# Two edits to a fused state-space mixer and MLP kernel: zero-padded bias rows, and a reordered opening

## The chip, the cores and the metric

The kernel runs on one core of one Trainium2 chip. The metric is device time in microseconds (us) of one execution; lower is better. The kernel before was run 7 times: median 574.7 us, from 574.32 to 580.91. One further number matters below: the execution that the profiler recorded took 574.59 us.

## What is computed

The input x has 2048 rows (tokens) of 1024 features. Two branches are computed from it and mixed by a gate per token:

```
g = sigmoid((x * gate_w).sum(-1))
a = S5(x):   Bu = x @ B_bar^T (complex);  h_t = Lam_bar * h_(t-1) + Bu_t;  a = 2 Re(h @ C^T) + x * Dskip
b = MLP(x):  gelu(layernorm(x) @ w1 + b1) @ w2 + b2        (1024 -> 3584 -> 1024)
out = g * a + (1 - g) * b
```

The bias b2 is a row of 1024 numbers that is added to every token's row of the second MLP product. In the kernel it is added on TensorE.

## The kernel before, in words

All work is recorded as tasks with an engine, an estimated duration, a priority and what they read and write. A planner (`Graph.schedule`) plays the tasks through its own estimates, and so fixes, before anything runs, one order of instructions for each engine: TensorE (PE), VectorE (DVE), ScalarE (ACT), GpSimd (POOL) and SyncE (SP, which issues most of the loads). On the chip each engine goes through its list in that order and waits at semaphores for what others must have done first. So an edit to a few tasks can move the order of many others.

The matrix products are done by a fast scheme with seven block products in place of eight. A group (`SG`) has seven parts `p1` to `p7`, each a run of K accumulating matmuls of 128x512 into a PSUM bank (`mm`, the matmuls of L828, which open an accumulation, and of L830, which add to one). Parts are interleaved between groups: a group's last parts run within the next group. Each group needs sums and differences of its operand blocks, which DVE makes (`dve_tt`, L882), and its results are moved out of PSUM by ACT and DVE.

The stages, in order of time:

- The **opening** (0 to about 25 us). SP issues loads of 128 rows each: rows of B (real and imaginary parts, `load_b`, L633 and L634) and of x (`load_x`, L621). PE transposes them with an identity, eight 128x128 transposes for one load: `t_x` for the first four loads of x (L650), `t_b` for the first four pairs of B (L666). Each set of eight fills one PSUM bank; DVE empties it for x (L654), ACT for B (L670). The banks come from `tbank()`, which gives bank 7 and bank 3 in turn. A row of small constants is transposed as well (`cst_T`, L684) and copied by DVE (L693); a chain of small DVE instructions on these constants follows. The first products of x and B (`bu_plain`) are woven in between the transposes of B, and `z_gate` (L1033, into bank 7) makes the gate's sums.
- The **bu stage** (to about 118 us): 14 groups of 28 matmuls, x times B. Meanwhile ACT, DVE and POOL do the layer norm, and DVE makes tables for the scan (L768).
- Four pairs of **m** and **b** stages (to about 468 us). An m stage is the first MLP product with gelu: 7 groups of 28 matmuls; DVE adds at L1275, ACT applies the gelu at L1271 and L1277. A b stage is the second product: 4 groups of 49 matmuls; DVE ends them at L1357. The first two pairs belong to the first half of the hidden features (`Fh == 0`), and only there b2 is added. In this time DVE also does the scan of the state-space branch (L1142, L1145, L1156), in 16 units, as filling between the work that PE waits for.
- The **y stage** (to the end): 8 groups of 56 matmuls with the scanned states and C, then out.

How b2 gets in: in each b group of the first half, part `p1` and part `p5` have one more matmul than the others. In `p1` its stationary operand is one row of 128 ones and its moving operand one row with the first half of b2; in `p5` they are two rows: (1, -1) and the two halves of b2. Both stationary operands are the first row or rows of the small tile STG, which `signs` (POOL, L687) overwrites once the constants have been transposed; the b2 rows lie in the buffer B2B, filled by two small loads (`em_b2`, L1557 and L1558). The lines:

```
v_one = View(V(STG, 0, [(1, 128)], npart=1), [b_stg])
v_sgn = View(V(STG, 0, [(1, 128)], npart=2), [b_stg])
st["A11"], mv["B11"] = st["A11"] + [v_one], mv["B11"] + [v_b2l]
st["S1"], mv["T1"] = st["S1"] + [v_sgn], mv["T1"] + [v_b2r]
```

B2B has had another use by then: the bu stage keeps one of its sums there (`US5`).

Of the kernel before, what the change touches and what calls it, by code (L numbers as in the profile page):

```python
# [412 lines left out]
def V(t, off, dims, npart=128):  # L413
    ps = 1
    for s in t.shape[1:]:
        ps *= s
    return bass.AP(t, off, [[ps, npart]] + [[a, b] for (a, b) in dims])


def build(nc, A_x, A_Lambda_re, A_Lambda_im, A_B_re, A_B_im, A_C_re, A_C_im, A_log_dt, A_Dskip,  # L420
          B_x, B_w1, B_b1, B_w2, B_b2, gate_w, out, stats=None):
    x2 = A_x[0]
    out2 = out[0]
    L, D = x2.shape
# [4 lines left out]
    DT = D // 128  # L429
# [14 lines left out]
    g = Graph()  # L444
    es = ExitStack()
    with es:
# [5 lines left out]
        def sem(name, dram=False):  # L452
            nsem[0] += 1
            return SemC(es.enter_context(nc.semaphore(name)), name, dram)
# [9 lines left out]
        STG = sb("stg", [128, 128], BF16)  # L464
        IDENT = sb("ident", [128, 128], BF16)
        ONESF = sb("onesf", [128, 128], F32)
# [61 lines left out]
        def tbank():  # L528
            return (7, 3)[nxt("tbank", 2)]
# [96 lines left out]
        def load_b(pt, prio):  # L626
            s = pt % 4

            v = AR.v(RX + s * 4096, [(1, 2 * D)])
            BN[pt] = v  # L630

            def em(e, pt=pt, s=s):
                i1 = e.dma_start(out=AR.v(RX + s * 4096, [(1, D)]).ap, in_=A_B_re[pt * 128:(pt + 1) * 128, :])  # L633
                i2 = e.dma_start(out=AR.v(RX + s * 4096 + 2048, [(1, D)]).ap, in_=A_B_im[pt * 128:(pt + 1) * 128, :])  # L634
                return [i1, i2]
            g.dma(prio, em, 2 * 128 * D * 2, ssem("bnat", s), writes=[v], name="bnat%d" % pt, ndma=2)
# [1 line left out]
        first_e = []  # L638
        first_a = []

        def t_x(k, prio):
            bk = tbank()
            v = XNAT[k]

            def em(e, k=k, bk=bk):
                ins = None
                base = XNAT[k].ap
                for dt in range(DT):
                    src = AR.v(XOFF(k) + dt * 256, [(1, 128)]).ap
                    ins = e.transpose(V(PS16[bk], dt * 128, [(1, 128)]), src, V(IDENT, 0, [(1, 128)]))  # L650
                return ins
            g.add("pe", 0.06 * DT, prio, em, reads=[v, b_ident], writes=[b_ps[bk]], name="xT_T%d" % k)
            o = AR.v(xqo(0, 0) + k * 256, [(512, DT), (1, 128)])
            first_e.append(g.add("dve", 0.65, prio, lambda e: e.tensor_copy(o.ap, V(PS16[bk], 0, [(128, DT), (1, 128)])),  # L654
                                 reads=[b_ps[bk]], writes=[o, b_ps[bk]], name="xT_e%d" % k))

        def t_b(pt, prio):
            s = pt % 4
            for ri in range(2):
                bk = tbank()  # L660

                def em(e, ri=ri, bk=bk):
                    ins = None
                    for dt in range(DT):
                        src = AR.v(RX + s * 4096 + ri * 2048 + dt * 256, [(1, 128)]).ap
                        ins = e.transpose(V(PS16[bk], dt * 128, [(1, 128)]), src, V(IDENT, 0, [(1, 128)]))  # L666
                    return ins
                g.add("pe", 0.06 * DT, prio, em, reads=[BN[pt], b_ident], writes=[b_ps[bk]], name="bT%d.%d" % (pt, ri))
                o = AR.v(bqo(pt, 2 * ri), [(1, D)])
                first_a.append(g.add("act", c_act(D), prio, lambda e, o=o, bk=bk: e.activation(o.ap, V(PS16[bk], 0, [(1, D)]), AF.Copy),  # L670
                                     reads=[b_ps[bk]], writes=[o, b_ps[bk]], name="bTe%d.%d" % (pt, ri)))

        load_b(0, (-0.95, 0))
        for k in range(4):
            load_x(k, (-0.9, k))
        for pt in range(1, 4):
            load_b(pt, (-0.85, pt))

        for k in range(4):
            t_x(k, (-0.8, k))  # L680
        t_b(0, (-0.79, 0))
        bk0 = tbank()
        g.add("pe", 0.06, (-0.75, 0),
              lambda e: e.transpose(V(PS16[bk0], 0, [(1, NROW)]), V(STG, 0, [(1, 128)], npart=NROW), V(IDENT, 0, [(1, NROW)], npart=NROW)),  # L684
              reads=[b_stg, b_ident], writes=[b_ps[bk0]], name="cst_T", extra=[g.tasks[-2]])
        g.add("pool", 0.4, P0,
              lambda e: e.affine_select(V(STG, 0, [(1, 128)], npart=2), V(ONESF, 0, [(1, 128)], npart=2), [[0, 128]], ALU.is_equal, -1.0,  # L687
                                        base=0, channel_multiplier=1),
              reads=[b_ones], writes=[b_stg], name="signs").slack = 4.0
        v_one = View(V(STG, 0, [(1, 128)], npart=1), [b_stg])  # L690
        v_sgn = View(V(STG, 0, [(1, 128)], npart=2), [b_stg])
        stage_names = ["LRE", "LIM", "LDT", "DSK", "B2", "GW", "B1"]
        cst_cp = g.add("dve", 0.15, P0, lambda e: e.tensor_copy(V(CST, 0, [(1, NROW)]), V(PS16[bk0], 0, [(1, NROW)])),  # L693
              reads=[b_ps[bk0]], writes=[bc(n) for n in stage_names] + [b_ps[bk0]], name="cst_copy")
# [484 lines left out]
        NP2 = FT // 4  # L1179
        b_acs = [B("acs%d" % k) for k in range(NTT)]  # L1180
        b_w1s = [B("w1s%d" % j) for j in range(FT // 2)]
        v_b2l = AR.v(B2B, [(1, 512)], npart=1)
        v_b2r = AR.v(B2B + 1024, [(1, 512)], npart=2)

        def xq(i, dt=None):
            if dt is None:
# [140 lines left out]
        def b_group(Fh, c, tp):  # L1327
            def hq(kh, t):
                return [ht(kh * HF + k, (2 * tp + t) * 128, 128) for k in range(HF)]

            def sq(i):
                return [AR.v(SQ + (tp + 1) % 2 * 7168 + i * 1792 + k * 256, [(1, 128)], FP16) for k in range(HF)]
            st = {"A11": hq(0, 0), "A12": hq(1, 0), "A22": hq(1, 1), "S1": sq(0), "S2": sq(1), "S3": sq(2), "S4": sq(3)}
            f = lambda i: [wq(i, k) for k in range(HF)]
            mv = {"B11": f(0), "B21": f(1), "B22": f(2), "T1": f(3), "T2": f(4), "T3": f(5), "T4": f(6)}
            if Fh == 0:

                st["A11"], mv["B11"] = st["A11"] + [v_one], mv["B11"] + [v_b2l]
                st["S1"], mv["T1"] = st["S1"] + [v_sgn], mv["T1"] + [v_b2r]
            o0 = [AO + nxt("bao", 4) * 4096 for _ in range(2)]  # L1340
            ov = [AR.v(o0[i // 2] + (i % 2) * 2048, [(1, 512)], F32) for i in range(4)]
            s5 = AR.v(AO + 16384, [(1, 512)], F32)
            k0 = c * 8 + 2 * tp
            gm = [(C("GM1", k0 + t), bc("GM1")) for t in range(2)]
            done = {}

            def fin(qd, q, bk):
                t = qd // 2
                o = ov[qd]
                nm = "%d.%d.%d" % (Fh, k0 // 2, qd)  # L1350
                sc = gm[t]
                sv = o if qd == 1 else s5
                if qd % 2 == 0:
                    g.add("act", c_act(512, ap_operands=1), (10.0, q + 1), lambda e: e.activation(o.ap, V(PS[bk], 0, [(1, 512)]), AF.Copy, scale=sc[0]),  # L1354
                          reads=[b_ps[bk], sc[1]], writes=[o, b_ps[bk]], name="ac" + nm)
                else:
                    g.add("dve", c_dve(512), (10.0, q - 2), lambda e: e.scalar_tensor_tensor(o.ap, V(PS[bk], 0, [(1, 512)]), sc[0], sv.ap, ALU.mult, ALU.add),  # L1357
                          reads=[b_ps[bk], sc[1], sv], writes=[o, b_ps[bk]], name="ac" + nm)
                done[qd] = True
                k = k0 + t  # L1360
                if done.get(2 * t) and done.get(2 * t + 1):
                    av = AR.v(o0[t], [(1, D)], F32)
                    if Fh == 0:
                        g.dma((10.0, q + 2), lambda e: e.dma_start(out=ACS[k], in_=av.ap), 128 * D * 4, ssem("ao", k % 4, True), reads=[av], writes=[b_acs[k]], name="acs%d.%d" % (Fh, k), q="pool")  # L1364
                    else:
                        g.dma((10.0, q + 2), lambda e: e.dma_start(out=ACS[k], in_=av.ap, accum_op=ALU.add), 128 * D * 4, ssem("ao", k % 4, True), reads=[av, b_acs[k]], writes=[b_acs[k]], name="acs%d.%d" % (Fh, k), q="pool")  # L1366
            return SG("_b%d.%d" % (Fh, k0 // 2), st, mv, fin, ov[1], s5, sc=[gm[0], gm[1]])
# [140 lines left out]
        for n, it in enumerate(flat):  # L1508
# [46 lines left out]
            if n == 0:  # L1555
                def em_b2(e):
                    return [e.dma_start(out=AR.v(B2B, [(1, D)], npart=1).ap, in_=bass.AP(B_b2.tensor, B_b2.offset, [[0, 1], [1, D]])),  # L1557
                            e.dma_start(out=AR.v(B2B + 1024, [(1, 512)], npart=1, p0=1).ap, in_=bass.AP(B_b2.tensor, B_b2.offset, [[0, 1], [1, 512]]))]  # L1558
                g.dma((40.0, 0), em_b2, 4096, sem("d_b2b"), writes=[v_b2l, v_b2r], name="b2b", ndma=2)
                w2_load(0)  # L1560
                for pg in range(PG):
                    for q in range(NQ):
                        ssm(pg, q)
# [80 lines left out]
```

## Time and profile before

| | |
|---|---|
| median of 7 runs | 574.7 us |
| the profiled execution: its own time / span from first to last instruction | 574.59 / 572.9 us |
| PE busy | 552.5 us, 96% of the span |
| DVE busy | 511.7 us, 89% |
| ACT busy | 279.7 us, 49% |
| POOL busy | 99.1 us, 17% |
| first transpose on PE | starts at 5.02 us |
| last matmul's result taken up by DVE | 565.65 us |

The busy time of PE counts overlapping matmuls once, and the end of a matmul is modelled, so the distance from one start to the next is the better measure of what a matmul costs. In the timeline, several like instructions are merged into one row: start, time from the first's start to the last's end, engine, line, and a count. A record can be missing.

### The profile page before, as it was taken

The numbers are of one execution on the slowest core, as the hardware profiler recorded it, in microseconds if no ns is written. First come the engines' busy times: TensorE is split into PE (matmuls) and PEld (weight loads), VectorE is DVE, ScalarE is ACT, GpSimd is POOL, SyncE is SP. The second block draws the span as 40 slices with busy tenths as digits, with TensorE's granted clock in tenths as the row PEclk, the third lists the DMA queues.
The fourth block names the chain that finished last, engine by engine and source line by source line (L and its number), as shares of the span: only waits on it lengthen the run. The fifth ranks groups of instructions, "written<-read, shape, count | busy, mean of one in ns | idle before, by whom it ended". The sixth has DMA issues, their size and how long they took to land.

```text
span 572.9 us, 7432 instructions
## 1 busy us (share of the span) xinstructions
PE 552.5 (96%) x2569; PEld 249.3 (44%) x2617; DVE 511.7 (89%) x865; ACT 279.7 (49%) x465; POOL 99.1 (17%) x159
## 2 busy tenths in 40 slices
PE   5899999999999999999999999999999999999994
PEld 4444444444334444444434444444444444444442
DVE  3899999999999999999999999999995878998652
ACT  2978999667652247662236673336662321111110
POOL 0024856630101010001211000210000210011000
PEclk9999999999999999999999999999999999999998
DMA  9975999889994766403878999899579999777501
GB/s 283 261 248 111 287 309 316 265 285 282 370 258 134 262 245 225 146 33 115 263 297 289 339 281 217 215 272 276 183 147 244 313 315 279 255 237 268 176 37 55
DMA packets 116675, 134.50 MB, mean 235 GB/s; under 512 B 70548, under 2 KB 92565, under 8 KB 115614
## 3 DMA queue, kind: packets, MB, share of 16 engines
q1 hardware_dynamic: 102548, 79.72, 50.1%
q0 software_dynamic: 13952, 54.29, 29.5%
q8 instruction: 20, 0.33, 0.2%
q14 instruction: 17, 0.14, 0.1%
q10 hardware_dynamic: 138, 0.02, 0.0%
HBM read 63.48 MB, written 54.80 MB: 206 GB/s over the span
## 4 chain that ended last, share of the span: by engine, by line
PE 82%; DVE 11%; issue 2%; ACT 2%; DMA 1%; SPq 0%; DVEq 0%; ACTq 0%
PE ps L830 57%; PE ps L828 24%; DVE ar L882 4%; DVE ar L1142 2%; DVE ar L1275 2%; DVE ar L1156 1%; DVE ar L1145 1%; ACT ar L670 1%; DMA ar<-in_A_x_dram 1%; PE ps L1033 1%; PE ps L650 0%; DVE ar L1357 0%; ACT ar L912 0%; ACT L720 0%; DVE ar L968 0%
## 5 line engine op out<-in xcount | busy, mean ns | idle before, releaser
L830 PE MATMUL ps<-ar 128*128 128x512 f16 (+1 forms) x1683 | 389.9, 379 | 4.1 <-DVE ar L1357 1.0
L830 PEld LDWEIGHTS ps<-ar 128*128 128x128 f16 (+1 forms) x1720 | 166.2, 98 | 207.3 <-issue 4.4
L828 PE MATMUL ps<-ar 128*128 128x512 bf16 (+1 forms) x741 | 181.7, 379 | 1.6 <-DVE ar L882 0.9
L882 DVE TENSOR_TENSOR ar<-ar 128x512 f16<-128x512 bf16 (+7 forms) x216 | 139.8, 685 | 8.2 <-PE ps L828 3.4
L828 PEld LDWEIGHTS ps<-ar 128*128 128x128 bf16 (+1 forms) x752 | 72.7, 98 | 90.3 <-DVE ar L882 3.5
L1156 DVE TENSOR_TENSOR_SCAN ar<-cst,init,ar 128x256 bf16<-128x256 f32 x128 | 87.9, 735 | 0.4
L846 ACT ACTIVATE ar<-ps 128x512 f32<-128x512 f32 x100 | 58.9, 593 | 48.1 <-PE ps L828 33.2
L1142 DVE TENSOR_TENSOR ar<-ar 128x2048 bf16<-128x2048 bf16 x64 | 77.2, 1218 | 0.0
L854 ACT ACTIVATE ps<-ps 128x512 f32<-128x512 f32 x66 | 38.5, 583 | 72.0 <-PE ps L828 71.8
L1271 ACT ACTIVATE ar<-ps,cst 128x512 bf16<-128x512 f32 x56 | 38.4, 686 | 25.9 <-PE ps L830 25.4
L847 ACT ACTIVATE ar<-ps,cst 128x512 f32<-128x512 f32 x32 | 22.0, 687 | 56.6 <-PE ps L828 35.8
L1354 ACT ACTIVATE ar<-ps,cst 128x512 f32<-128x512 f32 x32 | 22.0, 687 | 46.1 <-PE ps L830 46.1
L1277 ACT ACTIVATE ar<-ar,cst 128x512 bf16<-128x512 f32 x56 | 40.0, 715 | 8.5 <-DVE ar L1275 8.4
L1145 DVE TENSOR_TENSOR ar<-ar 128x1024 bf16<-128x1024 bf16 x64 | 42.3, 686 | 0.2
L1275 DVE TENSOR_TENSOR ar<-ps,ar 128x512 f32<-128x512 f32 x56 | 38.3, 684 | 2.7 <-PE ps L830 2.2
L897 POOL DMA_DIRECT2D scr_u<-ar x32 | 25.1, 785 | 52.2 <-ACT ar L912 18.0
L1357 DVE SCALAR_TENSOR_TENSOR ar<-ps,cst,ar 128x512 f32<-128x512 f32 x32 | 23.9, 748 | 11.2 <-PE ps L830 11.1
L1455 DVE SCALAR_TENSOR_TENSOR ar<-ps,cst,ar 128x512 bf16<-128x512 f32 x32 | 23.8, 749 | 9.7 <-PE ps L830 9.6
L1366 POOL DMA_DIRECT2D scr_ac<-ar x16 | 13.8, 881 | 81.2 <-issue 32.9
L1364 POOL DMA_DIRECT2D scr_ac<-ar x16 | 8.5, 532 | 100.6 <-DVE ar L882 47.7
L1462 POOL DMA_DIRECT2D out_dram<-ar x14 | 7.6, 544 | 83.4 <-DVE ar L1455 83.4
L1174 POOL DMA_DIRECT2D scr_h<-ar x16 | 9.6, 600 | 66.9 <-DVE ar L1145 66.7
(105 smaller groups left out, 262.5 us busy)
## 6 DMA issues: line engine op xcount, KB each, us to landing
scr_ac<-ar POOLq DMA_DIRECT2D x32, 512.0 KB, 7.4
scr_w<-ar POOLq DMA_DIRECT2D x14, 896.0 KB, 7.2
ar<-scr_w SPq DMA_DIRECT2D x14, 896.0 KB, 6.0
ar<-in_A_x_dram SPq DMA_DIRECT2D x32, 256.0 KB, 4.7
scr_u<-ar POOLq DMA_DIRECT2D x32, 256.0 KB, 4.7
ar<-scr_u SPq DMA_DIRECT2D x16, 512.0 KB, 5.8
scr_h<-ar POOLq DMA_DIRECT2D x16, 512.0 KB, 7.3
ar<-scr_ac SPq DMA_DIRECT2D x16, 512.0 KB, 6.6
```

Of the source, the lines that this page charges most:

```text
L828: ins = e.matmul(V(PS[bk], 0, [(1, n)]), st[i].ap, mv[i].ap, start=(i == 0), stop=(i == K - 1))
L830: ins = e.matmul(V(PS[bk], 0, [(1, n)]), st[i].ap, mv[i].ap, start=False, stop=(i == K - 1), skip_group_check=True)
L846: return e.activation(o.ap, V(PS[bk], 0, [(1, 512)]), AF.Copy)
L854: g.add("act", c_act(512), (pb[0], q - 2), lambda e: e.activation(V(PS[b], 0, [(1, 512)]), V(PS[a], 0, [(1, 512)]), AF.Copy), reads=[b_ps[ ...
L882: g.add("dve", c_tt16(n), (pb[0], q), lambda e: e.tensor_tensor(o.ap, a.ap, b.ap, op), reads=[a, b], writes=[o], name=nm, extra=ex).slack ...
L897: g.dma((1.0, q), lambda e: e.dma_start(out=US[pt // 4, :, 4 * pr:4 * pr + 4, r0:r0 + T], in_=evv.ap), 2 * 128 * CH * 2, ssem("us", 2 * ks ...
L1142: g.add("dve", c_tt16(UE), pri(i), lambda e: e.tensor_tensor(o.ap, a.ap, tbl.ap, ALU.mult), reads=[a, tbl], writes=[o], name=nm + tag)
L1145: g.add("dve", c_tt16(UE // 2), pri(i), lambda e: e.tensor_tensor(o.ap, a.ap, b.ap, op), reads=[a, b], writes=[o], name=nm + tag)
L1156: lambda e, pt=pt, ri=ri, vin=vin, go=go: e.tensor_tensor_scan(go.ap, Cb("R", pt, T), vin.ap, V(INIT, pt * 2 + ri, [(1, 1)]), ALU.mult, AL ...
L1271: g.add("act", c_act(512, ap_operands=1), (10.0, q + 1), lambda e: e.activation(o.ap, V(PS[bk], 0, [(1, 512)]), AF.Gelu_apprx_tanh, bias=C ...
L1275: g.add("dve", c_dve(512), (10.0, q - 2), lambda e: e.tensor_tensor(sv.ap, V(PS[bk], 0, [(1, 512)]), sv.ap, ALU.add), reads=[b_ps[bk], sv] ...
L1277: g.add("act", c_act(512, psum=False, ap_operands=1), (10.0, q + 3), lambda e: e.activation(o.ap, sv.ap, AF.Gelu_apprx_tanh, bias=C("B1", ...
```

## The change

There are two edits.

The first makes the b2 products full. `signs` now writes all 128 rows of STG: row 0 is ones, all others are minus one. The two moving operands are views of all 128 rows of B2B, which a new POOL instruction (`b2z`) clears before the b2 rows are loaded into rows 0 and 1. Both products use the same 128-row stationary operand; the zero rows add nothing.

The second reorders the opening. The loads of x 0 and x 1 are issued first, then B 0's real part, x 2, x 3, B 0's imaginary part; the two parts of B 0 are now separate loads with semaphores of their own. The transposes follow in the same order, each tied to the one before it, and use banks 7, 3, 1, 0, 7, 2; the constants go to bank 3. With `tbank()` starting afresh after them, the later transposes of B use banks 7, 3, 7, 3, 7, 3 where they used 3, 7, 3, 7, 3, 7.

```
-        def t_x(k, prio):
-            bk = tbank()
+        def t_x(k, prio, bk, ex):
...
-        def t_b(pt, prio):
+        def t_b(pt, prio, ris=(0, 1), bks=None, ex=()):
             s = pt % 4
-            for ri in range(2):
-                bk = tbank()
+            for ri in ris:
+                bk = bks[ri] if bks else tbank()
...
-                g.add("pe", 0.06 * DT, prio, em, reads=[BN[pt], b_ident], writes=[b_ps[bk]], name="bT%d.%d" % (pt, ri))
+                g.add("pe", 0.06 * DT, prio, em, reads=[AR.v(RX + s * 4096 + ri * 2048, [(1, D)]), b_ident], writes=[b_ps[bk]], name="bT%d.%d" % (pt, ri), extra=ex)
...
-        load_b(0, (-0.95, 0))
+        def load_b0(ri, ap):
+            v = AR.v(RX + ri * 2048, [(1, D)])
+            g.dma((-0.9, 1.5 + 2 * ri), lambda e: e.dma_start(out=v.ap, in_=ap[0:128, :]), 128 * D * 2,
+                  sem("d_b0%d" % ri), writes=[v], name="bnat0.%d" % ri)
+
+        load_b0(0, A_B_re)
+        load_b0(1, A_B_im)
+        BN[0] = AR.v(RX, [(1, 2 * D)])
...
-        for k in range(4):
-            t_x(k, (-0.8, k))
-        t_b(0, (-0.79, 0))
-        bk0 = tbank()
+        def last_pe():
+            return [t for t in g.tasks if t.eng == "pe"][-1:]
+
+        t_x(0, (-0.8, 0), 7, [])
+        t_x(1, (-0.8, 1), 3, last_pe())
+        t_b(0, (-0.8, 2), (0,), (1, 2), last_pe())
+        t_x(2, (-0.8, 3), 0, last_pe())
+        t_x(3, (-0.8, 4), 7, last_pe())
+        t_b(0, (-0.79, 0), (1,), (1, 2), last_pe())
+        bk0 = 3
...
-              lambda e: e.affine_select(V(STG, 0, [(1, 128)], npart=2), V(ONESF, 0, [(1, 128)], npart=2), [[0, 128]], ALU.is_equal, -1.0,
+              lambda e: e.affine_select(V(STG, 0, [(1, 128)]), V(ONESF, 0, [(1, 128)]), [[0, 128]], ALU.is_equal, -1.0,
...
-        v_one = View(V(STG, 0, [(1, 128)], npart=1), [b_stg])
-        v_sgn = View(V(STG, 0, [(1, 128)], npart=2), [b_stg])
+        v_sgn = View(V(STG, 0, [(1, 128)]), [b_stg])
...
-        v_b2l = AR.v(B2B, [(1, 512)], npart=1)
-        v_b2r = AR.v(B2B + 1024, [(1, 512)], npart=2)
+        v_b2l = AR.v(B2B, [(1, 512)])
+        v_b2r = AR.v(B2B + 1024, [(1, 512)])
+        v_b2 = AR.v(B2B, [(1, D)])
...
-                st["A11"], mv["B11"] = st["A11"] + [v_one], mv["B11"] + [v_b2l]
+                st["A11"], mv["B11"] = st["A11"] + [v_sgn], mv["B11"] + [v_b2l]
...
+                g.add("pool", 0.8, (39.0, 0), lambda e: e.memset(v_b2.ap, 0.0), writes=[v_b2], name="b2z")
                 g.dma((40.0, 0), em_b2, 4096, sem("d_b2b"), writes=[v_b2l, v_b2r], name="b2b", ndma=2)
```

More of the change, by code (lines that the diff above doesn't have):

```diff
@@ L651, in em @@
                 return ins
-            g.add("pe", 0.06 * DT, prio, em, reads=[v, b_ident], writes=[b_ps[bk]], name="xT_T%d" % k)
+            g.add("pe", 0.06 * DT, prio, em, reads=[v, b_ident], writes=[b_ps[bk]], name="xT_T%d" % k, extra=ex)
             o = AR.v(xqo(0, 0) + k * 256, [(512, DT), (1, 128)])
@@ L677, in build @@
             load_b(pt, (-0.85, pt))
-        for k in range(4):
-            t_x(k, (-0.8, k))
-        t_b(0, (-0.79, 0))
-        bk0 = tbank()
+        def last_pe():
[7 more added lines that the diff above has]
+        bk0 = 3
         g.add("pe", 0.06, (-0.75, 0),
               lambda e: e.transpose(V(PS16[bk0], 0, [(1, NROW)]), V(STG, 0, [(1, 128)], npart=NROW), V(IDENT, 0, [(1, NROW)], npart=NROW)),
-              reads=[b_stg, b_ident], writes=[b_ps[bk0]], name="cst_T", extra=[g.tasks[-2]])
+              reads=[b_stg, b_ident], writes=[b_ps[bk0]], name="cst_T", extra=last_pe())
         g.add("pool", 0.4, P0,
-              lambda e: e.affine_select(V(STG, 0, [(1, 128)], npart=2), V(ONESF, 0, [(1, 128)], npart=2), [[0, 128]], ALU.is_equal, -1.0,
+              lambda e: e.affine_select(V(STG, 0, [(1, 128)]), V(ONESF, 0, [(1, 128)]), [[0, 128]], ALU.is_equal, -1.0,
                                         base=0, channel_multiplier=1),
               reads=[b_ones], writes=[b_stg], name="signs").slack = 4.0
-        v_one = View(V(STG, 0, [(1, 128)], npart=1), [b_stg])
-        v_sgn = View(V(STG, 0, [(1, 128)], npart=2), [b_stg])
+        v_sgn = View(V(STG, 0, [(1, 128)]), [b_stg])
         stage_names = ["LRE", "LIM", "LDT", "DSK", "B2", "GW", "B1"]
```

## The prediction

> **What bounds the kernel now.** I read the engines' shares first, then who PE waits for, then the time of groups with and without b2, then the opening instruction by instruction. The shares:
>
> ```profile
> PE 552.5 (96%) x2569; PEld 249.3 (44%) x2617; DVE 511.7 (89%) x865; ACT 279.7 (49%) x465; POOL 99.1 (17%) x159
> ```
>
> PE is full, and DVE not far behind. All waits of PE that the profile names:
>
> ```profile
> PE ps L650 <- DMA ar<-in_A_x_dram: 5.6, 2, 5.0
> PE ps L1033 <- DVE ar L768: 1.4, 1, 1.4
> PE ps L830 <- DVE ar L1357: 1.0, 1, 1.0
> PE ps L828 <- DVE ar L882: 0.9, 2, 0.5
> PE ps L830 <- DVE ar L882: 0.8, 3, 0.3
> ```
>
> 5.6 us go by until x has landed, 1.4 at the first gate product, 2.7 on DVE. Nothing else holds PE, so between 5 us and its last matmul time can only be won from PE's own instructions or from the opening. Now PE in the first b stage, from the timeline (start, length, line, shapes, count):
>
> ```profile
> 174.97 1.67 PE L828 MATMUL ps<-ar 128*128 128x512 f16 x7
> 176.58 0.38 PE L828 MATMUL ps<-ar,stg 2*128 2x512 bf16 x1
> 176.89 6.22 PE L830 MATMUL ps<-ar 128*128 128x512 f16 x28
> ```
>
> and the windows of one b group of the first half and one of the second (length, PE busy, matmuls, clock, DMA):
>
> ```profile
> 175.13:186.55 11.42, 11.37 (x52) 1.00 0.52 162
> 352.09:362.67 10.58, 10.53 (x50) 1.00 0.74 196
> ```
>
> The group without b2 takes 10.58 us for 49 matmuls: 0.2159 each. The group with b2 has 51, which at that pace are 11.01; it takes 11.42, so 0.41 too much, 0.205 per b2 product. The rows above show where: seven matmuls from 174.97 should hand over at 176.48, but the two-row product starts at 176.58, and its successor 0.31 after it instead of 0.216. About 0.10 is lost on the way in and 0.10 on the way out. The opening:
>
> ```profile
> 5.02 1.03 PE L650 MATMUL ps<-ident,ar 128*128 128x128 bf16 x8 [5.02 <-DMA ar<-in_A_x_dram]
> 6.64 2.85 PE L650 MATMUL ps<-ident,ar 128*128 128x128 bf16 x24 [0.58 <-DMA ar<-in_A_x_dram]
> 9.40 1.91 PE L666 MATMUL ps<-ident,ar 128*128 128x128 bf16 x16
> 11.53 0.24 PE L684 MATMUL ps<-ident,stg 76*128 76x76 bf16 x1 [0.22 <-ACT ar L670]
> 12.00 1.71 PE L828 MATMUL ps<-ar 128*128 128x512 bf16 x7 [0.22 <-issue]
> ...
> 23.15 1.89 PE L1033 MATMUL ps<-ar,gwc 128*2 128x512 bf16 x16 [1.43 <-DVE ar L768]
> ...
> 19.65 1.95 ACT L670 ACTIVATE ar<-ps 128x1024 bf16<-128x1024 bf16 x2
> 21.94 1.06 ACT L670 ACTIVATE ar<-ps 128x1024 bf16<-128x1024 bf16 x1
> ```
>
> PE starts with x 0, which is the third load; x 2, x 3 and both halves of B 0 need a bank that is still being emptied; the first product (eight matmuls, one record missing) starts near 11.7. The gate product's wait is put down to DVE, but it writes bank 7, and the last transpose of B was emptied from bank 7 by ACT until 23.0: that is the wait.
>
> [...] here 90 ns for the one- and two-row loads against a mean of 98, so full rows bring no new load time. [...] In the trace the opening transposes follow each other at about 0.10 us until 11.5 and at about 0.055 ((1.06 - 0.24)/15) from 13.5, though the clock column shows 1.00 throughout. [...]
>
> **The change, part by part.**
>
> *b2 products.* 8 groups x 2 = 16 products x 0.205 = **3.3 us** off PE. Bounds: 0, if the loss has to do with the tile STG and not with the rows; 3.3, if the products become ordinary. I take 3.3, since the one-row (bf16 beside bf16) and two-row (bf16 beside fp16) products lose the same, which excludes the type.
>
> *POOL.* `signs` on 128 rows: the like instruction for the identity took 0.28, the two-row one 0.28: nothing. `b2z`: POOL memsets took 0.20 for 128 fp32 and 0.10 for 16, so 0.9 ns an element, an estimate of 0.9 us for 1024[...]. It waits for the last use of B2B (DVE, 124.75), then the b2 loads on SP wait for it: from 124.78 they move to about 125.8. Behind them on SP now stands the load of scan unit 3 (121.26 before, ahead of them): about 126.5, landing 5.8 later at 132.3; its reader, L1142, starts at 152. The w2 load behind goes out at 129.3 anyway. On POOL one u store (125.34) moves by 0.9; its readers come far later. b2 itself is needed at 163.7. All hidden; uncovered it would be 1 us once.
>
> *Opening loads.* The landings before, by place in SP's list, from issue time and time to landing: 3.7, 4.35, 5.0, 6.6, 7.3, 8.0 us (first 0.80 + 2.9, third 1.72 + 3.3, sixth 3.19 + 4.8). Same sizes, same twelve loads ahead of the first DMA transpose, so I keep these landings: x 0 3.7, x 1 4.35, B real 5.0, x 2 6.6, x 3 7.3, B imaginary 8.0. PE at 0.86 per eight[...]: 3.75 to 6.35 for the first three, 6.6 to 9.2 for the others without a bank wait (bank 7 is empty again long before), constants to 9.4. x 3 is copied by DVE 8.55 to 9.25; the first product starts at about 9.45 in place of 11.7: 2.2 us. [...]
>
> *Banks.* The last transposes of B now go to bank 3, and the gate product waits for the eviction before it, which ended near 21.5 in place of 23.0. Then the last transpose itself (to 21.7) is the limit: 1.4 us more. x by DMA transpose, which the gate also needs, was issued at 6.88 and takes 7.8: landed long before 19.5.
>
> Opening together: 2.2 + 1.4 - 0.5 = **3.1 us** (bounds 2.0 and 3.6). DVE's own chain starts with the constants at 9.5 in place of 11.8, 2.3 earlier; the remaining 0.8 has to come out of its idle waits before 118, some 4.6 us.
>
> *What is late next.* DVE. The window in which PE loses most (length, then busy time of PE, weight loads, DVE, ACT and POOL):
>
> ```profile
> 142.00:164.00 22.00, 21.00 (x94) 8.62 (x94) 21.90 (x34) 14.54 (x24) 2.12 (x4) 1.00 1.10 338
> ```
>
> Here DVE has 0.1 us free in 22. PE lost 0.7 to DVE between 142 and 167, and 1.6 between 290 and 341. From 167 to 290, where PE gets the 3.3 us faster, DVE waited for PE 3.9 us, so it can follow, but not everywhere at the right moment. Bounds: 0 and 3.3 given back; I take 0.9.
>
> Sum: 3.3 + 3.1 - 0.9 = 5.5. On the profiled execution 574.6 - 5.5 = 569.1 (span 572.9 - 5.5 = 567.4, and 1.7 around it); the median stands 0.1 above that execution, so **569.2**.
>
> **Rivals.**
>
> *b2 without effect* (the loss is STG's or stays hidden): 574.7 - 3.1 = 571.6. For it: nothing in the trace shows a full-row product from STG. Against: both shapes lose exactly at the switch. Chance 0.10.
>
> *DVE becomes the bound* and gives back the b2 gain, by 290 at the latest: 574.7 - 3.1 = 571.6, as in the case above. For it: 0.1 us free in 22. Against: 3.9 us of waits for PE just where the gain falls. Chance 0.12.
>
> *The opening isn't faster:* the loads land at the pace of the DMA engines whatever the order[...]. Against: place 1 was measured at 3.7. 574.7 - 3.3 + 0.9 for DVE = 572.3. Chance 0.08.
>
> *Slower:* the planner's new order puts fillers of the scan in front of evictions in the first and third m stages, the two in which PE waited before. In the new order two L1142 (1.2 us each) of the first scan unit stand together ahead of an addition of the bu stage where there was one. If each of these 14 groups loses one scan instruction (L1156, 0.735 us), it costs 10.3, so 574.7 - 6.4 + 10.3 = 578.6; it decides against the change from 6.4/14 = 0.46 us per group. Against: between 25 and 118 us PE waited for nothing, with DVE almost as full. Chance 0.05.
>
> **How the numbers follow.** Main case 0.65 at 569.2, its own range 567.0 to 571.0. 0.5% of 574.7 is 2.9 us: faster means below 571.8, and this is about what a measurement of this kernel can tell from no change. Main case nearly all faster (0.64); b2 without effect 0.06; DVE bound 0.07; slow opening 0.03; with fewer losses than I counted (under 567) hardly anything to add: faster 0.80, same 0.15, slower 0.05. The range: the main case's bounds and the three rivals up to 572.4, which leaves the slower rival above and the chance that old waits on DVE vanish too (2.3 us more) below: 566.4 to 572.4.
>
> **What would show it.** b groups of the first half at 11.0 us, b2 products 0.216 from start to start; first transpose near 3.75; first product near 9.45; gate product near 19.7; PE's waits on DVE at most 3.6. Wrong if the b groups stay at 11.4 (b2), if the first product is at 9.5 but PE's matmuls are 0.43 apart for over 1 us (clock), or if waits on DVE exceed 5 us (DVE).

## The result: the gain is there and a collision of transfers takes it back

| | before | changed kernel |
|---|---|---|
| median of all runs | 574.8 us (64 runs) | 578.6 us (27 runs) |
| fastest to slowest run | 573.4 to 581.4 us | 569.7 to 595.9 us |
| the profiled execution: time / span | 574.59 / 572.9 us | 581.17 / 579.4 us |
| PE busy, share of the span | 552.5 us, 96% | 549.9 us, 95% |

The ratio, 0.9986 with a 95% interval of 0.9965 to 1.0007, is taken over the runs within 1.5% of each kernel's fastest, which of the changed kernel are 12 of the 27, with a median of 574.9 us, while the profile below is of one of its longer runs. Even the shorter runs bring no gain, then, and only the fastest, 569.7, comes near the prediction, 569.2. The typical run is 3.8 us slower than before, and the spread has grown from 8 to 26 us.

The opening and the b2 products did what was predicted. The opening of the changed kernel, in the timeline of PE (start, length, line, shapes, count):

```profile
3.71 1.86 PE L649 MATMUL ps<-ident,ar 128*128 128x128 bf16 x16 [3.71 <-DMA ar<-in_A_x_dram]
...
9.79 1.67 PE L839 MATMUL ps<-ar 128*128 128x512 bf16 x7 [0.53 <-DVE cst L704]
...
19.41 1.89 PE L1044 MATMUL ps<-ar,gwc 128*2 128x512 bf16 x16
```

The first transpose starts at 3.71 (5.02 before), and the gate product at 19.41 (23.15 before) without a wait. Seven matmuls in 1.67 us are 0.215 apart. The b2 products, same view:

```profile
175.47 0.38 PE L839 MATMUL ps<-ar,stg 128*128 128x512 bf16 x1
175.68 6.21 PE L841 MATMUL ps<-ar 128*128 128x512 f16 x27
...
183.24 0.38 PE L839 MATMUL ps<-ar,stg 128*128 128x512 bf16 x1
```

The matmul after a b2 product now starts 0.21 us later, not 0.31. What PE waits for (us in total, times, longest):

```profile
PE ps L841 <- ACT ps L865: 9.1, 1, 9.1
PE ps L649 <- DMA ar<-in_A_x_dram: 3.7, 1, 3.7
PE ps L841 <- ACT ar L857: 2.1, 1, 2.1
```

The first and the third line are new. The first wait lies in the bu stage, where the kernel before had none; the third lies in the y stage, before 504.63 us, and is not followed here. The windows show the place of the first: the kernel before (length, busy time of PE, weight loads, DVE, ACT and POOL with counts, clock, DMA share, GB/s), then the changed kernel. The DMA share is the time that packets took, over the span of 16 engines, so it can exceed 1.

```profile
80.00:90.00 10.00, 9.95 (x48) 4.51 (x47) 10.00 (x20) 8.91 (x20) 4.22 (x7) 1.00 1.11 320
90.00:95.00 5.00, 5.00 (x25) 2.27 (x24) 4.97 (x12) 4.53 (x9) 4.63 (x6) 1.00 1.17 313
95.00:100.00 5.00, 4.95 (x24) 2.27 (x24) 5.00 (x9) 4.89 (x10) 2.72 (x5) 1.00 0.98 344
```

```profile
80.00:90.00 10.00, 9.95 (x47) 4.56 (x47) 9.35 (x19) 6.54 (x14) 5.86 (x9) 1.00 1.23 180
90.00:95.00 5.00, 1.60 (x8) 0.51 (x6) 0.00 (x0) 0.00 (x0) 0.00 (x0) 0.89 1.26 117
95.00:100.00 5.00, 0.00 (x0) 0.00 (x0) 2.57 (x5) 3.05 (x6) 0.98 (x2) 0.50 1.05 208
100.00:105.00 5.00, 4.13 (x12) 1.67 (x14) 4.38 (x9) 3.90 (x10) 2.54 (x4) 0.59 1.22 236
```

From 92 to 97 us PE, DVE, ACT and POOL all stand, and PE until 100.65. The DMA engines are busier than before already from 80 to 90 us (share 1.23 against 1.11), while they move 180 GB/s where they moved 320. The chain of waits of the changed kernel through this place (start, length, what):

```profile
79.44 17.97 DMA scr_u<-ar
97.41 0.02 issue
97.43 0.06 DVE ar L979
...
98.97 1.15 ACT ar L999 x2
100.11 0.50 ACT ps L865
100.61 0.05 issue
100.65 1.89 PE ps L841 x4
```

The stores of u values issued between 60 and 110 us (shortest, median and longest time to landing), before and then in the changed kernel:

```profile
DMA to landing us min/median/max: 2.8/5.3/6.3
```

```profile
DMA to landing us min/median/max: 4.3/5.0/18.2
```

Four of the 14 in the changed kernel are late, two pairs issued from 78.7 and 84.6: they take 15.7 to 18.2 us. The u evictions have only two buffers in turn, and so an eviction of ACT waits until the first of these stores has landed:

```profile
ACT ar L968 <- DMA scr_u<-ar: 9.9, 1, 9.9
```

DVE (L979) waits 8.0 us for the second, the one in the chain. Behind the eviction on ACT, with row statistics (L999) and one more eviction in between, stands the seed (L865), with which ACT fills a bank ahead of PE's additions, and for it PE waits. What else is under way then? The queue of SP, in the timeline; before:

```profile
73.88 6.83 SPq L1197 DMA_TRANSPOSE ar<-scr_xn  x2
80.81 1.19 SPq L1228 DMA_DIRECT2D ar<-in_B_w_dram  x1
84.91 5.87 SPq L1197 DMA_TRANSPOSE ar<-scr_xn  x2
```

and in the changed kernel:

```profile
70.91 0.39 SPq L1241 DMA_DIRECT2D ar<-in_B_w_dram  x1
73.08 30.85 SPq L1210 DMA_TRANSPOSE ar<-scr_xn  x4
```

These are the first four DMA transposes of the normalized rows (`xn_load`), 512 KB each. Before, they went out in pairs of 6.83 and 5.87 us, with the first load of w1 between them. Now the w1 load comes first, and the four take 30.85 us in one stretch. From issue to landing they take 15.1 us in the median, where they took 6.5.

No edit touches these transposes. But the planner fixes the order of every engine from its own estimates, and the edit to the opening changed these. Behind the opening 112 instructions stand in another place: 65 on DVE, 31 on ACT, 13 on POOL, 3 on SP. On POOL the stores of normalized rows (L1021) now lie among the u stores (L908): the first four rows used to be stored one after the other between 65.2 and 67.8 us, and are now stored from 64.3 to 69.9, and the next four follow at 72.5 to 75.4, just as the transposes begin. Before, the next four went out at 77.2 to 79.6, while the first pair of transposes was under way.

### The profile page after: what moved, and what is told of

Its sections match the earlier page's. It is cut to its first block, busy times and chain, and to the rows that moved or that the text cites. A ratio compares the mean times of both kernels' runs of the same rounds, so it can differ in the third digit from the quotient of the medians.

```text
span 579.4 us, 7430 instructions
## 1 busy us (share of the span) xinstructions
PE 549.9 (95%) x2569; PEld 250.8 (43%) x2617; DVE 511.8 (88%) x865; ACT 279.9 (48%) x465; POOL 98.2 (17%) x160
## 4 chain that ended last, share of the span: by engine, by line
PE 71%; DVE 14%; DMA 8%; issue 3%; ACT 2%; SPq 0%; POOL 0%; DVEq 0%; ACTq 0%
PE ps L841 49%; PE ps L839 21%; DMA scr_u<-ar 4%; DVE ar L893 4%; DMA ar<-in_A_x_dram 2%; DVE ar L1153 2%; DVE ar L1156 1%; DVE ar L1288 1%; DVE ar L1447 1%; DVE ar L1167 1%; DMA ar<-in_A_B_re_dram 1%; ACT ar L999 1%; PE ps L665 1%; PE ps L1044 1%; DVE ar L1019 1%
## 5 line engine op out<-in xcount | busy, mean ns | idle before, releaser
L841 PEld LDWEIGHTS ps<-ar 128*128 128x128 f16 (+1 forms) x1720 | 167.9, 98 | 219.9 <-ACT ps L865 9.7
L893 DVE TENSOR_TENSOR ar<-ar 128x512 f16<-128x512 bf16 (+7 forms) x216 | 140.0, 685 | 4.9 <-PE ps L841 2.2
L1153 DVE TENSOR_TENSOR ar<-ar 128x2048 bf16<-128x2048 bf16 x64 | 77.2, 1219 | 0.5 <-ACT ar L807 0.4
L865 ACT ACTIVATE ps<-ps 128x512 f32<-128x512 f32 x66 | 38.5, 584 | 69.6 <-PE ps L839 63.1
L908 POOL DMA_DIRECT2D scr_u<-ar x32 | 25.3, 793 | 60.7 <-DVE ar L974 17.9
L1370 DVE SCALAR_TENSOR_TENSOR ar<-ps,cst,ar 128x512 f32<-128x512 f32 x32 | 23.9, 748 | 10.1 <-PE ps L841 7.4
L968 ACT ACTIVATE ar<-ps 128x512 bf16<-128x512 f32 x28 | 16.7, 596 | 16.8 <-DMA scr_u<-ar 9.9
```

What stands on the lines that cost most here:

```text
L841: ins = e.matmul(V(PS[bk], 0, [(1, n)]), st[i].ap, mv[i].ap, start=False, stop=(i == K - 1), skip_group_check=True)
L865: g.add("act", c_act(512), (pb[0], q - 2), lambda e: e.activation(V(PS[b], 0, [(1, 512)]), V(PS[a], 0, [(1, 512)]), AF.Copy), reads=[b_ps[ ...
L893: g.add("dve", c_tt16(n), (pb[0], q), lambda e: e.tensor_tensor(o.ap, a.ap, b.ap, op), reads=[a, b], writes=[o], name=nm, extra=ex).slack ...
L908: g.dma((1.0, q), lambda e: e.dma_start(out=US[pt // 4, :, 4 * pr:4 * pr + 4, r0:r0 + T], in_=evv.ap), 2 * 128 * CH * 2, ssem("us", 2 * ks ...
L1153: g.add("dve", c_tt16(UE), pri(i), lambda e: e.tensor_tensor(o.ap, a.ap, tbl.ap, ALU.mult), reads=[a, tbl], writes=[o], name=nm + tag)
```

## The experiments

The letters in the expectations: O, the new order of instructions; T, the earlier start of the stage, whatever the order; P, the first store of w1 sums on POOL, now amid the transposes; Q, the first w1 load on SP, now ahead of all four. The kernel before ran beside each set; its median there was 575.1 to 575.5 us, its longest run 579.7 to 590.4.

**The two edits apart.** The b2 edit alone, the opening alone:

```
b2_only:   before.py + v_sgn on 128 rows, v_b2l / v_b2r on 128 rows, b2z
open_only: before.py + load_b0, t_x / t_b with fixed banks, cst_T in bank 3
```

> The kernel before with the b2 edit alone; the order of instructions on every engine stays as before, but for the added clearing of the b2 buffer on POOL. If the 16 products become ordinary ones, each group of the first half's b stages takes 11.0 us in place of 11.42 and the whole about 571.5 (3.3 us less), less what DVE gives back (at most to 574.8). If the loss had to do with the tile STG, groups stay at 11.42 and the time at 574.8.

> The changed kernel with b2 as before; orders are those of the changed kernel. All theories put the stall near 85 to 100 us on this edit, so it should be there: gate product at 19.4 us as in the changed kernel, then PE waiting for a seed that ACT makes late, in most executions. Median 3 us above that of the changed kernel, about 580, with a wide spread; and 571 in an execution without the stall.

b2 alone: 573.3 us, ratio 0.9969 (0.9954 to 0.9984), so 1.8 us faster. The gain in PE's own work is larger, but PE waited 3.3 us for DVE in place of 2.7, and 0.9, in the y stage, for an eviction of ACT (L845) that does not appear in the list of before. Its order is that of before, but for the added clearing. The opening alone: 586.7 us in the median, from 574.5 to 591.4. So the loss comes with the opening edit, and with it comes the new order. This is 8 us above the changed kernel, where 3 were expected, and is not explained. Its profile is of a short run, 576.7 us, and shows the stall in a milder form: the four transposes take 24.4 us in one stretch and land after 11.7 us in the median, and PE waits 3.2 us for seeds, 0.9 of it in the bu stage.

**One moved transfer at a time**, in the changed kernel and in the one before:

```
after_sp:   SP:   w1_0 (first w1 load) behind xnT0.0.1, the second transpose
after_pool: POOL: w1s0 (first store of w1 sums) behind ln_nmr2, as before
before_sp:  SP:   w1_0 ahead of all four transposes, as in the changed kernel
```

> The changed kernel, but on SP the first w1 load stands behind the first two transposes of the normalized rows, as before the change, in place of ahead of all four. Theory Q (that load ahead of four transposes in a row is what slows the u stores): stall gone, 569 to 570 with the spread of the kernel before. Theory P (the first w1 store on POOL falls among the transposes) and theory T (earlier timing alone): no change, median 578 and the wide spread.

> The changed kernel, but on POOL the first store of w1 (896 KB) stands where it stood before the change, behind the third layer-norm chain, about 10 us later, after the transposes. Theory P: stall gone or down to 2 us, 569 to 571. Theories Q and T: no change, median 578 and the wide spread; the u store issued before the w1 store is as late as in the changed kernel (18 us).

> The kernel before with one move: the first w1 load goes on SyncE ahead of all four transposes of the normalized rows, so that the transposes are issued with no load between them. Theory Q (it is this place on SyncE alone that lets four transposes pile up): 577 to 584 us, four transposes over 20 us. Theory T, and theory O where the stores' order on GpSimd is what matters: 574.5 to 576 us, transposes about 13 us.

P is not needed for the stall: with the store at 90.6 us in place of 83.0 the four transposes took 39.0 us, PE waited 15.9 us for seeds, the median was 581.3, and a store of rows under way from 74.7 already took 12.7 us to land. The store still falls among the transposes there, so this does not show it to be harmless. after_sp doesn't decide on Q. The pairs were apart again and took 10.1 and 8.8 us, and PE waited only 0.6 us for a seed, but DVE, whose new order has the w1 sums early, now stood waiting for the late load, issued at 84.8 and landed at 92.7, and PE waited 7.6 us for ACT behind it: 579.1 us. before_sp is the cleaner test: four transposes in one stretch take 15.5 us there, and the median is 575.9, ratio 1.0016 (1.0003 to 1.0030). Two of its 13 runs were over 578 us, and three of 35 of the kernel before beside it. Q alone explains little.

**The order against the early start.** The whole order is exchanged, both ways. Each entry names an engine, a task, and the task that it now goes behind; the kernel before gets the reverse moves:

```
         g.schedule(horizon=HORIZON)
+        for mv in (("act", "ln_sq1", "ln_sq0"), ("act", "ln_sq4", "s5_u3.0"),
...
+            ("pool", "xns0", "us1.1.1"), ("pool", "xns1", "xns0"),
...
+            ("sp", "w1_0", "xnT0.0.1"), ("sp", "ul0.3", "w1_3")):
+            move(*mv)
```

> The changed kernel, whole, with the order of the kernel before put back on ScalarE, VectorE, GpSimd and SyncE behind the opening (112 instructions moved; the opening's loads, transposes and banks and the b2 products stay as changed). Theory O (the planner's new order sends the transposes of the normalized rows, the row stores and the u stores into each other): the four transposes take about 13 us in two pairs again, no wait of TensorE for ScalarE's seed is over 3 us, and the time is about 569 us, narrow. Theory T (the early start alone does it, whatever the order): as the changed kernel, 574 to 581 us with a wide spread, four transposes over 20 us.

> The kernel before with its own opening and b2 products, but with the order of the changed kernel on ScalarE, VectorE, GpSimd and SyncE behind the opening. Theory O: the transposes collide here too, over 20 us for the four, and the time is 576 to 584 us, wide. Theory T: no collision, 574 to 576 us as before, give or take the 1 us that an order not meant for this opening costs.

This settles it. The changed kernel with the old order: 568.2 us, all five runs between 567.7 and 570.9, ratio 0.9886 (0.9869 to 0.9903). The kernel before with the new order: 581.8 us, from 574.9 to 592.3. T falls, O stands. With the old order, what PE waits for, and SP's queue:

```profile
PE ps L649 <- DMA ar<-in_A_x_dram: 3.8, 2, 3.5
PE ps L839 <- DVE ar L893: 1.3, 3, 0.5
...
PE ps L841 <- ACT ps L865: 0.2, 1, 0.2
```

```profile
70.43 7.02 SPq L1210 DMA_TRANSPOSE ar<-scr_xn  x2
77.55 1.22 SPq L1241 DMA_DIRECT2D ar<-in_B_w_dram  x1
82.82 6.73 SPq L1210 DMA_TRANSPOSE ar<-scr_xn  x2
```

In the bu stage PE waits for no seed, although the stage starts as early as in the changed kernel; the 0.2 us lie at 128 us, behind it. The span of this profile is 566.4 us, 13.0 less than that of the changed kernel. The wait for the seed (9.1), the slow start after it (an estimate of 1.7, worked out in the last section) and the wait in the y stage (2.1) are nearly all of this. In the kernel before with the new order:

```profile
PE ps L830 <- ACT ps L854: 9.9, 1, 9.9
```

```profile
75.83 33.93 SPq L1197 DMA_TRANSPOSE ar<-scr_xn  x4
```

the same stall, with the old opening.

**Which engine's order?** In each run the order of before is put back on some engines only, by the same moves.

> The changed kernel with the order of before put back behind the opening on GpSimd alone (13 stores and statistics moved); VectorE, ScalarE and SyncE keep the new order. If the place of the row stores among the u stores is what lets the transposes collide: 567 to 570 us, narrow, as with all four orders back. If VectorE's order (which decides when the rows are ready) is the cause: 574 to 582 us, wide, and four transposes over 20 us.

> The changed kernel with the order of before put back behind the opening on VectorE alone (65 instructions moved). If VectorE's order is the cause: 567 to 571 us, narrow. If GpSimd's order of the stores is: 574 to 582 us, wide, with a wait of TensorE for ScalarE's seed of 5 us or more.

> The changed kernel with the order of before put back behind the opening on ScalarE alone (31 instructions, the row statistics and table factors among the u evictions). If ScalarE's order is without effect: as the changed kernel, 574 to 582 us, wide. If it has made the rows or the evictions late: below 572 us.

> The changed kernel with the order of before put back behind the opening on VectorE and GpSimd, SyncE (first w1 load ahead of the four transposes) and ScalarE as changed. If only the two together make it, 567 to 570 us here, and over 574 us in both runs with one alone. If SyncE's or ScalarE's order has a part in it, over 572 us here.

> The changed kernel with the order of before on VectorE, GpSimd and SyncE behind the opening; only ScalarE keeps the new order. If the place of the first w1 load on SyncE carries what was left when VectorE and GpSimd alone were put back (575.2 us): 567 to 570 us. If ScalarE's order carries it: 573 to 576 us.

> The changed kernel with the order of before on ScalarE, VectorE and GpSimd behind the opening; only SyncE keeps the new order (first w1 load ahead of the four transposes). If SyncE's order carries what was left: 573 to 577 us, four transposes of 15 us or more in one stretch. If ScalarE's order carries it: 567 to 570 us.

| old order on | runs | median, us | fastest to slowest, us | over 578 us |
|---|---|---|---|---|
| none (the changed kernel) | 27 | 578.6 | 569.7 to 595.9 | 15 |
| POOL | 22 | 576.9 | 573.8 to 579.6 | 4 |
| DVE | 22 | 576.1 | 573.6 to 580.4 | 2 |
| ACT | 22 | 576.9 | 568.9 to 590.5 | 10 |
| DVE, POOL | 22 | 575.2 | 571.8 to 595.3 | 7 |
| DVE, POOL, SP | 22 | 575.3 | 570.9 to 587.4 | 6 |
| ACT, DVE, POOL | 17 | 571.3 | 568.1 to 585.1 | 4 |
| all four | 5 | 568.2 | 567.7 to 570.9 | 0 |

I had expected one engine to carry it, and none does. POOL's or DVE's old order alone takes away the longest runs but not the loss; ACT's alone leaves the spread; with SP's order alone still new, or ACT's alone still new, runs over 578 us remain. ACT's old order added to DVE's and POOL's brings most, from 575.2 to 571.3. With five runs the last row cannot say how rare such long runs are, and an order mixed from two plans can bring waits of its own, so which of the moves are needed stays open.

**Are the transposes the cause, or only a sign?** In after_plain and before_plain the same four transfers are plain loads of the same rows and bytes. The rows then stand untransposed, and what is made of them is something else; these two kernels are for timing alone. The edit holds for the first half of the rows (`c == 0`), so it also replaces the four transposes with which these rows are loaded again near 335 us. Shortened:

```
-  e.dma_start_transpose(out=o.ap, in_=XNS[r0:r0 + 512, dh * 512:(dh + 1) * 512])
+  e.dma_start(out=o.ap, in_=bass.AP(XNS.tensor, XNS.offset + r0 * D + dh * 512,
+                                    [[D, 128], [128 * D, 4], [1, 512]]))    # c == 0 only
```

> The changed kernel in its own new order, but the first four transposes of the normalized rows are plain loads of the same rows and the same 512 KB into the same places (so the rows stand untransposed in them and the first half of the rows' products computes something else). If the slow transposes are what holds up the u stores: no wait for ScalarE's seed over 3 us, the four loads land within some 6 us each, and the time is 566 to 571 us, narrow. If the new order costs by itself (late evictions, early w1 sums): 574 to 581 us still.

> The kernel before with the first four transposes of the normalized rows replaced by plain loads of the same rows and bytes (the rows stand untransposed, so the first half of the rows' products computes something else). If the kernel before pays nothing for its transposes: 574 to 575.5 us, and the pure gain of the change is then the difference to the changed kernel with plain loads, 569.3 us. If it pays for them too: below 573.5 us.

The changed kernel with plain loads, in its own new order: 569.3 us, from 568.2 to 569.7, ratio 0.9898 (0.9877 to 0.9920). No wait of PE for a seed is left in its list, and SP's queue has:

```profile
70.83 0.39 SPq L1245 DMA_DIRECT2D ar<-in_B_w_dram  x1
73.05 10.35 SPq L1212 DMA_DIRECT2D ar<-scr_xn  x4
```

The loads landed 8.9 us after issue in the median, not within 6 as expected, but no u store took more than 8.2. The kernel before gains nothing by plain loads: 575.2, ratio 0.9991 (0.9974 to 1.0007). So the cause is the transposes in the new order: the new order costs nothing that shows when they are plain loads, and the old order costs nothing with them. What it is in a transpose is not separated: from 68 to 108 us the changed kernel's transfers go in 11,706 packets, 9,211 of them under 512 bytes, with plain loads in 7,743, and 787 of them under 512, so it may be the transposing or the many small packets. The difference of the two kernels without these transposes, 575.2 - 569.3 = 5.9 us (5.4 by their ratios), is the change's own gain.

**One transpose at a time**, in the changed kernel, each waiting until the one before has landed:

```
+        xt = [t for t in g.order["sp"] if t.name.startswith("xnT0.")]
+        for a, b in zip(xt, xt[1:]):
+            b.deps.add(a)
```

> The changed kernel in its own new order, with one more wait on SyncE: each of the first four transposes of the normalized rows is issued only when the one before it has landed. If the transposes slow one another (four in flight at once) and through that the stores: each lands within some 6 us, the last by about 100 us, no wait of TensorE for ScalarE's seed over 3 us, and the time is 567 to 572 us, narrow. If it is a transpose beside the stores of rows and u values that is slow, however few are in flight: over 574 us and wide, as the changed kernel, or slower for the late rows.

Neither expectation fits whole. The median is 576.6, the slowest run 580.4 (595.9 in the changed kernel), the transposes land after 7.3 us in the median in place of 15.1, and no u store takes over 9.2. PE still waits, the second line in the bu stage, the first behind it, at 128 us:

```profile
PE ps L841 <- ACT ps L865: 3.4, 1, 3.4
PE ps L841 <- ACT ar L857: 2.1, 2, 1.6
```

So the long stall is gone. But the last transpose is now issued at 102.6, and DVE then waits 4.8 us for its rows (L893): the wait is only elsewhere. And the first of the four, issued at 73.7 with no other transpose in flight, still took 14.1 us, where it took 12.6 in the changed kernel and 5.2 in the kernel before; the other three took less, with 7.3 as the median of the four. So this transpose didn't need others beside it to be slow. Issued close about the first are two stores of u values and four of rows, from 72.1 to 75.8; in the kernel before two of u values go out from 74.9, and the rows from 77.2, when the first transpose has nearly landed. That these stores slow it is not tested by itself. How much the transposes slow one another, and which of the stores suffers or disturbs most, stays open as well.

## Why the prediction was wrong

- *b2 products*: right in what they cost. A product takes 0.21 us from start to start, and two like products of successive groups (183.24 and 194.25) are 11.01 apart, the predicted 11.0. Its weight load takes 98 ns with full rows, the mean of the others too, where those of one and two rows took 90. Alone, the edit brought 1.8 us where the step counted 3.3 less what DVE gives back: the waits for DVE and ACT above. Why a product of one or two rows lost 0.10 us on either side no run shows; the runs show that with full rows the loss is gone.
- *POOL and the b2 loads*: hidden, as predicted; `b2z` took 0.95 us for 0.9, and PE has no wait for it or the loads.
- *Opening loads*: right. 3.71 for 3.75, and 9.5 to 9.8 for 9.45 (one record of eight is missing). The 0.5 us taken off, for matmuls 0.43 apart at the start, was the author's estimate, and it was not lost: eight transposes from 6.15 us take 1.03, eight from 8.62 only 0.61, and the matmuls are 0.215 apart from the first. The clock column shows 1.00 here too, for the slower transposes as for the faster.
- *Banks*: right and somewhat too small. The gate product at 19.41 for 19.7; opening together 3.7 us for 3.1.
- *What is late next. DVE.* This is the step that failed. The giving back by DVE was sized about right: with the old order PE waits 3.5 us for DVE against 2.7 before, 0.8 for the 0.9 taken. But DVE was not what was late next. It was a store of u values, 18.2 us under way beside the transposes on SP, and behind it the seed, for which PE waited 9.1 us in the profiled run. The step looked only at the engines' free time, and the prediction at transfers only in the opening and around b2. Against its slower rival it held that "between 25 and 118 us PE waited for nothing", which is true of the old order. The new order, which is fixed before anything runs, puts four transposes in a row and the row stores into one stretch; the cost of that order on the DMA queues was put at nothing, without a reason.
- *The rival that is slower* gave 578.6, the measured median, by another mechanism: scan instructions ahead of evictions in the m stages. PE's waits on DVE behind the opening, 3.4 us in all in the changed kernel next to 2.7 before, exclude it, since it needed 10.3; the number is a coincidence. Its first half, that the planner's new order does the damage, was right.

The sum itself holds where the order is held: 6.6 us of gain measured (575.1 x (1 - 0.9886)), 5.5 predicted; 568.2 for 569.2. In that profile the gate product starts at 18.82, so the opening brought 4.3 us for the 3.1 counted; that is the difference and a little more. The prediction's list of PE's waits before leaves out two of 0.2 us each; nothing rests on them.

## What to carry to other kernels

Where a planner fixes the order, compare the two orders on every engine and in every DMA queue, far from the edit as well, before counting a gain; and run an edit once with the old order held, which tells the edit from the shuffle. Price a DMA transpose in the order in which it will run, since its time in another may not hold (here 15.1 us in the median for 6.5), and ask which eviction has to wait when the stores next to it land late (here after 18.2 us, with ACT waiting 9.9). When the spread of the runs grows, as here from 8 to 26 us, look for transfers that sometimes meet. Here the changed kernel with the old order is the one to keep: 568.2 us, faster than both.

## What was not expected of the hardware

The same four DMA transposes are cheap in one order and dear in another. In the kernel before, the 512 KB of each land in 6.5 us in the median, and with plain loads in their place the kernel's time is the same (575.2 us, and 575.5 beside it). In the changed kernel's order the same four took 15.1 us in the median, plain loads in the same places 8.9, and u stores beside the transposes took up to 18.2 us, beside the plain loads up to 8.2. What a transpose took in the one order did not tell what it takes in the other.

After the stall PE starts slowly. In the changed kernel its last matmul before the stall ends at 91.6 us. The clock column, in narrower windows, shows 1.00 to about 93.9, 0.50 from there to about 104.1, 3.45 us after the first matmul at 100.65, and then 1.00. Meanwhile the matmuls are 0.43 us apart: four at 100.65 take 1.89 us, where four at 105.81, 0.216 apart, take 1.03. At half pace these 3.45 us lose half of their length, an estimate of 1.7 us, so this stall of 9.1 us cost more than its length. What brings the clock down, and up again, is not shown by one stall.
